# Matmuls on 48 of 64 rows and columns of a tile: the delta-rule state in a DeltaNet and SwiGLU kernel

## The chip, the cores and the metric

The kernel runs on one core of one Trainium2 chip. The metric is the device time of one execution in microseconds (us), as the median of several runs.

## What is computed

Two layers follow each other. The first is a DeltaNet recurrence over 768 positions for 4 batches x 8 heads with head size D = 48; its outputs, put side by side, are the 3072 rows of 384 that a SwiGLU feed-forward layer (384 to 1536 and back) takes, after an RMS normalization. Everything is float32.

```python
k_n = k / (norm(k, axis=-1) + 1e-06)
state = zeros((B, H, D, D))
for t in range(S):
    kt, vt, bt = k_n[:, :, t], v[:, :, t], beta[:, :, t, None]
    y[:, :, t] = einsum('bhd,bhde->bhe', q[:, :, t], state)
    v_old = einsum('bhde,bhd->bhe', state, kt)
    state = state + bt[..., None] * einsum('bhd,bhe->bhde', kt, vt - v_old)
...
x = y.transpose(0, 2, 1, 3).reshape(B * S, H * D)
xn = x / sqrt(mean(x * x) + 1e-06) * rms_g
g = xn @ w_gate
out = (g * sigmoid(g) * (xn @ w_val)) @ w_out
```

## The kernel before, in words

**Chunks.** The 768 positions are cut into NCH = 12 chunks of C = 64. Within a chunk the recurrence becomes matrix products: the inverse of a triangular matrix of each head is built (`prep`, lines 577 to 815), partly with matmuls, partly by a substitution on VectorE (lines 693 and 699) fed by DMAs that turn the layout over DRAM. Then `recur(c)` (lines 818 to 1030) does the part that needs the state: `on_state` (lines 834 to 844) multiplies the transposed keys `kt` by the state, line 854 subtracts that from the values, `mr` (line 886) applies the inverse and gives `u_`, `on_state` is used once more for the queries `qt`, `pu` (line 900) adds what lies within the chunk, and `ku` (lines 1011 to 1019) forms keys-transposed times `u_`, which line 1028 adds to `state` (in chunk 0, line 1030 copies it there).

**Heads and tiles.** There are 32 heads (batch x head). `k2`, `q2` and `state` hold two heads per free index, one on partitions 0 to 63 and one on 64 to 127. For the keys the partition is the position in the chunk, and a head's 48 values lie in DP = 64 columns of which the last 16 are set to zero once at the start (line 375). `turn` (line 509) transposes keys and queries on TensorE, so in `kt` and `qt` each head has 64 partitions, of which the last 16 hold these zeros. The state of a head is 48 columns on 64 partitions; its last 16 partitions hold zeros because the padded columns of K do.

**The matmuls concerned.** `ku` is 32 matmuls per chunk, for chunks 0 to 10: stationary operand `kn[rows, x_]` (64 positions x 64 columns), moving operand `u_[rows, x_]` (64 x 48), output on 64 partitions x 48 columns. `on_state` is 32 matmuls per call, called twice per chunk for chunks 1 to 11: stationary `t[rows, u, ...]` (64 rows x 64 positions), moving `state[rows, 2u+g]` (64 rows x 48), output 64 x 48. Both use TensorE as four tiles of 64 x 64: the loops' two innermost indices walk through the four combinations of upper or lower rows and upper or lower columns, and the two banks that a call fills belong to the upper and the lower rows.

**The feed-forward layer.** Chunks 0 and 1 are computed plainly (`ffn_plain`, lines 1064 and 1046). For later chunks the products are formed with fewer multiplications out of sums of blocks (`ffn`, line 1157 with sums on VectorE in line 1167; `down`, line 1214). In the first 125 us the weights arrive as 64-bit numbers and are turned into float32 on ScalarE and VectorE (`weights`, lines 440 to 480).

**The order of the work.** Each step is entered with `P.add(engine, duration, function, priority, ...)`. The planner (`Plan`, lines 60 to 243) simulates the engines with these written durations, tries 60 orders and issues the best one, engine by engine[...]. The durations are written numbers: 0.98 us for `ku` (line 1022) and for each `on_state` (lines 851 and 859). Before 70 us idle TensorE time is filled with dummy products (line 1312).

Of the kernel before, what the change touches and what calls it, by code (L numbers as in the profile page):

```python
# [246 lines left out]
def kernel(  # L247
# [17 lines left out]
    nc = tc.nc  # L265

    B, H, S, D = q.shape
# [12 lines left out]
    def sbt(name, shape, n=None, dt=FP32):  # L280
        if n is None:
            return sb.tile(shape, dt, name=name)
        return [sb.tile(shape, dt, name=f"{name}{i}") for i in range(n)]
# [45 lines left out]
    u_ = sbt("u", [128, 16, D])  # L329
# [212 lines left out]
    def kkeys_(c):  # L542
        return [("k2", c % NK, 0), ("k2", c % NK, 1)]
# [274 lines left out]
    def recur(c):  # L818
# [3 lines left out]
        kn = k2[c % NK]  # L822
# [7 lines left out]
        if c:  # L830

            psk, psq = [Group(), Group()], [Group(), Group()]

            def on_state(t, ps):
                for x_ in range(4):
                    for g in range(2):
                        for d in range(2):
                            for bb in range(2):
                                rows, u, n = slice(64 * d, 64 * d + 64), 4 * bb + x_, 96 * x_ + 48 * g
                                nc.tensor.matmul(  # L840
                                    ps[d].t[64 * bb : 64 * bb + 64, n : n + 48],
                                    t[rows, u, 64 * g : 64 * g + 64],
                                    state[rows, 2 * u + g],
                                )

            def by_d(t, d):

                return t.rearrange("s (x d n) -> s x d n", x=4, d=2)[:, :, d]

            P.rows = 64  # L850
            P.add("PE", 0.98, lambda: on_state(kt[ikq], psk), pr, r=ktk + sk, w=psk + rk, ps=psk, size=128)
            P.rows = 128
            for d in range(2):
                P.add("DVE", V(384), lambda d=d: nc.vector.tensor_tensor(  # L854
                    out=by_d(r_.rearrange("s h e -> s (h e)"), d), in0=by_d(vt.rearrange("s h e -> s (h e)"), d),
                    in1=psk[d].t[:, 0:DM].rearrange("s (x n) -> s x n", x=4), op=ALU.subtract,
                ), pr, r=vk + [psk[d]], w=[("r", d)], last=psk[d])
            P.rows = 64
            P.add("PE", 0.98, lambda: on_state(qt, psq), pr, r=qk + sk, w=psq, ps=psq, size=128)
            P.rows = 128  # L860
            for d in range(2):
                P.add("ACT", A(384), lambda d=d: nc.scalar.copy(
                    by_d(yn.rearrange("s p n -> s (p n)"), d), psq[d].t[:, 0:DM].rearrange("s (x n) -> s x n", x=4)
                ), py, r=[psq[d]], w=[("yn", p) for p in range(2)], last=psq[d])
# [44 lines left out]
        def uk(h):  # L909
            return [("u", bb, p) for bb in range(2) for p in h]  # L910
# [97 lines left out]
        if c < NCH - 1:  # L1008
            pss = [Group(), Group()]

            def ku():
                for b in range(B):
                    for j in range(2):
                        for d in range(2):
                            for g in range(2):
                                rows = slice(64 * g, 64 * g + 64)
                                x_ = 4 * b + 2 * j + d
                                n = 48 * (2 * b + j)
                                nc.tensor.matmul(pss[g].t[64 * d : 64 * d + 64, n : n + 48], kn[rows, x_], u_[rows, x_])  # L1019

            P.rows = 64
            P.add("PE", 0.98, ku, py + 2, r=kkeys_(c) + [("k2p", c % NK)] + uk((0, 1)), w=pss, ps=pss, size=128)
            P.rows = 128
            for g in range(2):
                dst = state[:, g:16:2]
                src = lambda g=g: pss[g].t[:, 0:DM].rearrange("s (u e) -> s u e", e=D)
                if c:
                    P.add("DVE", V(384), lambda dst=dst, f=src: nc.vector.tensor_tensor(out=dst, in0=dst, in1=f(), op=ALU.add), py + 2, r=[pss[g]], w=[("st", g)], last=pss[g])
                else:
                    P.add("ACT", A(384), lambda dst=dst, f=src: nc.scalar.copy(dst, f()), py + 3, r=[pss[g], ("xp", 0), ("xp", 1)], w=[("st", g)], last=pss[g])  # L1030
# [315 lines left out]
```

## Time and profile before

| what | value |
|---|---|
| median of 3 runs | 718.07 us (716.91 to 720.38) |
| the profiled execution, its own time | 720.75 us |
| its span, first to last instruction | 719.0 us |
| TensorE (PE) busy | 701.6 us, 98% of the span |
| PE weight loads (PEld) busy | 652.8 us |
| VectorE (DVE) busy | 553.8 us, 77% |
| ScalarE (ACT) busy | 314.3 us, 44% |
| mean granted TensorE clock | 0.993 |
| matmul records of line 1019 (`ku`) | 704, busy 12.8 us |
| matmul records of line 840 (`on_state`) | 2 x 704, busy 12.6 and 12.5 us |

A float32 matmul stands in the trace as two pairs of a weight load (LDWEIGHTS, engine PEld) and a MATMUL (engine PE), so the 32 matmuls of one call are 64 records. Records overlap: a MATMUL record lasts about 218 ns while the next one starts some nanoseconds later, so the time that a group takes is read from where the next group starts, not from the mean of one record. A shape such as `64*64 64x48` is active rows * active columns of the stationary operand, then rows x columns of the moving operand.

### The profile page before, as it was taken

Reading aid. Unit: us, or ns where it says so; the run is one execution under the profiler, and the core shown is the slowest. Engines: PE = TensorE matmul, PEld = TensorE weight load, DVE = VectorE, ACT = ScalarE, POOL = GpSimd, SP = SyncE. Lnnn points to the kernel's source line nnn. Section 1 sums busy time; section 2 is a strip of 40 time slices with the busy share of each in tenths; the row PEclk is TensorE's granted clock in tenths of the full one; section 3 lists DMA queues with packets and bytes.
Section 4 is the critical chain, followed back from the end, with each engine's and each line's share of the span. In section 5 each row is a group of like instructions: output and inputs, shape, how many; then the busy total and the mean of one; then the engine's idle time right before and its main releaser. Section 6 shows DMA issues by size and latency. Waiting matters only on the chain.

```text
span 719.0 us, 23540 instructions
## 1 busy us (share of the span) xinstructions
PE 701.6 (98%) x10178; PEld 652.8 (91%) x10178; DVE 553.8 (77%) x1128; ACT 314.3 (44%) x732; POOL 152.1 (21%) x150
## 2 busy tenths in 40 slices
PE   8988999999999999999999999999999999999997
PEld 7787877777799999998999999999999999999997
DVE  4898989998967958946967967975968958847473
ACT  5514544232345436354345255355355354344331
POOL 4200307004314132203213303203203221000000
PEclk9998999999999999999999999999999999999999
DMA  8867698141154261242234253253152061040000
GB/s 172 208 127 169 141 251 233 23 66 43 35 87 80 39 111 27 46 73 59 57 58 78 44 95 55 40 86 65 38 106 48 13 115 28 13 65 2 23 1 23
DMA packets 210071, 54.68 MB, mean 76 GB/s; under 512 B 199216, under 2 KB 202288, under 8 KB 209968
## 3 DMA queue, kind: packets, MB, share of 16 engines
q1 hardware_dynamic: 205120, 52.26, 36.4%
q8 instruction: 80, 1.31, 0.8%
q10 hardware_dynamic: 4848, 0.92, 0.7%
q14 instruction: 23, 0.19, 0.1%
HBM read 40.83 MB, written 12.32 MB: 74 GB/s over the span
## 4 chain that ended last, share of the span: by engine, by line
PE 79%; DVE 12%; DMA 4%; issue 2%; SPq 1%; POOL 1%; ACT 1%; ACTq 0%; DVEq 0%; POOLq 0%
PE bank L1157 36%; PE bank L1214 19%; PE bank L1064 6%; PE bank L1046 3%; PE bank L532 3%; PE bank L840 2%; PE bank L509 2%; DVE acc L699 2%; DMA more<-in_moe_w_gate_dram 2%; PE bank L799 2%; PE bank L886 1%; PE bank L1019 1%; PE bank L900 1%; DVE w_in L480 1%; DVE acc L693 1%
## 5 line engine op out<-in xcount | busy, mean ns | idle before, releaser
L1167 DVE TENSOR_TENSOR tmp<-tmp,bank 128x512 f32<-128x512 f32 x180 | 122.0, 685 | 85.9 <-PE bank L1157 75.9
L1157 PE MATMUL bank<-xf,w_in 128*128 128x128 f32 x1440 | 181.5, 277 | 0.2 <-DVE tmp L1167 0.2
L1157 PEld LDWEIGHTS bank<-xf,w_in 128*128 128x128 f32 x1440 | 169.8, 192 | 2.6 <-DVE tmp L1167 0.6
L1157 PE MATMUL bank<-xf,more 128*128 128x128 f32 x960 | 124.7, 277 | 0.0
L1157 PEld LDWEIGHTS bank<-xf,more 128*128 128x128 f32 x960 | 115.6, 192 | 1.7 <-DVE tmp L1167 0.4
L1169 ACT COPY tmp<-bank 128x512 f32<-128x512 f32 x120 | 68.5, 584 | 82.1 <-PE bank L1157 57.2
L699 DVE TENSOR_REDUCE acc<-acc 128x30 f32<-128x90 f32 (+4 forms) x180 | 85.1, 473 | 6.2
L1173 ACT ACTIVATE tmp<-tmp 128x256 f32<-128x256 f32 x120 | 49.7, 417 | 87.9 <-DVE tmp L1167 87.5
L693 DVE TENSOR_TENSOR acc<-acc,at 128x60 f32<-128x60 f32 (+4 forms) x180 | 63.4, 352 | 8.7 <-POOL at L676 5.9
L1214 PE MATMUL bank<-wo_sb,hf 128*128 128x192 f32 x360 | 63.8, 328 | 0.0
L1174 DVE TENSOR_TENSOR hf<-tmp 128x256 f32<-128x256 f32 x120 | 51.8, 443 | 13.0 <-ACT tmp L1173 11.7
L1214 PEld LDWEIGHTS bank<-wo_sb,hf 128*128 128x128 f32 x360 | 58.2, 190 | 0.3
L646 POOL TENSOR_TENSOR at<-at,beta_b 128x1024 f32<-128x1024 f32 x10 | 25.6, 2555 | 146.1 <-DMA at<-dkk 146.1
L554 POOL TENSOR_TENSOR knrm<-ksum,half 128x16 f32<-128x16 f32 x12 | 35.9, 2991 | 33.4 <-DVE ksum L553 33.4
L720 POOL COPY acc<-acc 128x128 f32<-128x128 f32 x40 | 17.1, 458 | 116.9 <-DVE acc L699 116.1
L1312 PE MATMUL bank<-ident 128*128 128x128 f32 x298 | 40.3, 296 | 1.4 <-POOL ident masks.py:199 1.4
L1312 PEld LDWEIGHTS bank<-ident 128*128 128x128 f32 x298 | 38.1, 209 | 2.5 <-POOL ident masks.py:199 1.4
L1046 PE MATMUL bank<-wo_sb,hf 128*128 128x384 f32 x96 | 34.3, 491 | 0.3 <-DVE r L854 0.3
L1064 PE MATMUL bank<-xf,w_in 128*128 128x256 f32 x144 | 33.6, 382 | 0.0
L1064 PE MATMUL bank<-xp,w_in 128*128 128x256 f32 x144 | 33.4, 383 | 0.0
L1064 PEld LDWEIGHTS bank<-xf,w_in 128*128 128x128 f32 x144 | 26.8, 190 | 4.9
L1064 PEld LDWEIGHTS bank<-xp,w_in 128*128 128x128 f32 x144 | 26.7, 190 | 4.4 <-issue 0.2
(164 smaller groups left out, 1047.9 us busy)
## 6 DMA issues: line engine op xcount, KB each, us to landing
at<-dkk SPq DMA_DIRECT2D x23, 256.0 KB, 4.0
q<-in_q_dram SPq DMA_DIRECT2D x24, 192.0 KB, 3.8
more<-in_moe_w_gate_dram SPq DMA_DIRECT2D x6, 768.0 KB, 6.0
more<-in_moe_w_val_dram SPq DMA_DIRECT2D x6, 768.0 KB, 7.2
more<-in_moe_w_out_dram SPq DMA_DIRECT2D x6, 768.0 KB, 8.4
vt<-in_v_dram SPq DMA_DIRECT2D x24, 192.0 KB, 4.2
out_dram<-tmp SPq DMA_DIRECT2D x48, 96.0 KB, 2.2
k<-in_k_dram SPq DMA_DIRECT2D x23, 192.0 KB, 4.2
```

What stands on the lines that cost most here:

```text
L554: P.add("POOL", 2.95, lambda: nc.gpsimd.tensor_tensor(out=knrm[i2], in0=ksum[i2], in1=half, op=ALU.pow), pn, r=[("ksum", i2), "half"], w=[ ...
L693: nc.vector.tensor_tensor(out=acc[:, 1:3, 0:n, j + 2 : W].rearrange("p a i t -> p i a t"), in0=acc[:, old, 0:n, j : j + 2, None].to_broadc ...
L699: nc.vector.tensor_reduce(out=acc[:, new, 0:n, j + 2 : W], in_=acc[:, lo : lo + 3, 0:n, j + 2 : W].rearrange("p a i t -> p i t a"), axis=A ...
L1046: nc.tensor.matmul(po[p].t[:, 0:DM], hf[:, spot(f), 128 * p : 128 * p + 128], wo_sb[:, spot(f)], start=(f == f0), stop=(f == f1 - 1), skip ...
L1064: nc.tensor.matmul(ps.t[:, TOK * side : TOK * side + TOK], w_in[:, side, h_, 3 * t + i_, n : n + 128], x_[:, 2 * t : 2 * t + 2].rearrange( ...
L1157: nc.tensor.matmul(g.t[:, 128 * z : 128 * z + 128], fac[:, side, 128 * f : 128 * f + 128], xf[:, xs], start=(begin and z == 0), stop=False ...
L1167: P.add("DVE", V(512), lambda t=t, g=g: nc.vector.tensor_tensor(out=t, in0=t, in1=g.t, op=ALU.add), -1, r=[g], w=[tk], last=g)
L1169: P.add("ACT", A(512), lambda t=t, g=g: nc.scalar.copy(t, g.t), -1, r=[g], w=[tk], last=g)
L1173: P.add("ACT", A(256), lambda t=t: nc.scalar.activation(out=t[:, 0:256], in_=t[:, 0:256], func=ACTF.Silu), -1, w=[tk])
L1174: P.add("DVE", V(256), lambda t=t, f0=f0, p=p: nc.vector.tensor_tensor(out=hf[:, spot(f0) : spot(f0) + 2, 128 * p : 128 * p + 128], in0=t[ ...
L1214: nc.tensor.matmul(g.t[:, 0:192], a_[:, f], b_[:, f], start=(begin and f == 0), stop=(f == 5), skip_group_check=True)
L1312: nc.tensor.matmul(warm[:, 0:128], ident, ident)
```

## The change

`ku` takes 48 columns of K instead of 64 as its stationary operand and writes 48 instead of 64 partitions of the bank. `on_state` contracts over 48 rows instead of 64: both the transposed keys or queries and the state are read on partitions 0 to 47 and 64 to 111. Its stationary operand still has 64 columns, and its output is as before. The padding of `k2` and `q2` is still set to zero, the transposes still turn 64 columns, and lines 1028 and 1030 still move all 128 partitions into `state`; the 16 partitions after each head's 48 then hold whatever the bank held, and no matmul reads them.

```diff
@@ on_state @@
-                                rows, u, n = slice(64 * d, 64 * d + 64), 4 * bb + x_, 96 * x_ + 48 * g
+                                rows, u, n = slice(64 * d, 64 * d + D), 4 * bb + x_, 96 * x_ + 48 * g
                                 nc.tensor.matmul(
                                     ps[d].t[64 * bb : 64 * bb + 64, n : n + 48],
                                     t[rows, u, 64 * g : 64 * g + 64],
@@ ku @@
-                                nc.tensor.matmul(pss[g].t[64 * d : 64 * d + 64, n : n + 48], kn[rows, x_], u_[rows, x_])
+                                nc.tensor.matmul(pss[g].t[64 * d : 64 * d + D, n : n + D], kn[rows, x_, 0:D], u_[rows, x_])
```

The instruction lists of the two kernels have the same length and order on all five engines, with the same waits. They differ in 1056 matmuls: 352 of line 1019 with the narrower stationary operand and output, 704 of line 840 with fewer rows. In both lists these matmuls are assigned to tiles of 64 x 64 at the same positions.

## The prediction, made before the changed kernel ran

> **What bounds the kernel now.** I read the page's busy table first, then the table by stretches of time, then the chain of work that ended last, and last the groups by shape.
>
> ```profile
> PE 701.6 (98%) x10178; PEld 652.8 (91%) x10178; DVE 553.8 (77%) x1128; ACT 314.3 (44%) x732; POOL 152.1 (21%) x150
> ```
>
> TensorE is busy 98% of the span. Overlapped records can hide idle spots in such a share, so the table by stretches says where it holds:
>
> ```profile
> 60.00:128.00 68.00, 64.88 (x1189) 52.66 (x1187) 62.39 (x98) 35.78 (x84) 20.66 (x13) 0.97 0.77 185
> 128.00:200.00 72.00, 72.00 (x637) 55.45 (x638) 66.23 (x133) 21.20 (x51) 17.44 (x17) 1.00 0.23 42
> 200.00:500.00 300.00, 298.55 (x4804) 289.26 (x4803) 225.47 (x478) 142.71 (x335) 72.61 (x71) 1.00 0.37 65
> 500.00:719.00 219.00, 214.35 (x2885) 208.84 (x2883) 153.27 (x327) 89.65 (x216) 29.20 (x34) 1.00 0.22 40
> ```
>
> The first number after the stretch's length is PE's busy time, the third VectorE's. From 128 us on PE is idle for moments only, until the last outputs are stored. Before 128 us VectorE is the fuller engine (62.4 of 68 us) with weight conversion, and PE's time there has dummy products in it (line 1312). So a microsecond of PE work saved after 128 us should come off the end, and one saved before is likely hidden. The chain agrees: from 60 to 128 us it is mostly VectorE conversion, after that mostly PE.
>
> Now the matmuls that change. These are pieces of the chain (start, length, both in us):
>
> ```profile
> 371.30 10.02 PE bank L1157 x88
> 381.32 2.01 PE bank L840 x128
> 398.63 1.08 PE bank L1019 x64
> 400.65 2.15 PE bank L1214 x12
> ```
>
> A call of 64 records takes 1.08 us; two calls of `on_state` one behind the other take 2.01, so the second costs 0.93 us. Four records on four tiles are one round, a call is 16 rounds, and 0.93 / 16 is 58 ns a round. The single starts in the trace say the same: four MATMULs start within 20 ns, the next four 58.3 ns later (58.29 to 58.36 in nearly every call of lines 1019, 840, 886, 900 and 532). Only the first round of a call behind 128-row work is longer, 93 to 94 ns. What sets 58.3? Line 532 moves 64 columns and lines 1019 and 840 move 48, at the same 58.3; all load 64 stationary columns. Line 1157 (128 stationary, 128 moving) takes 111.66 ns from start to start within a group (10.02 us / 88 = 113.9 ns with the entry into it). From 64 to 128 columns is 53.3 ns, 0.833 ns a column, with 5 ns over. Lines with moving operands wider than their weights follow another line: 162.5 ns at 192 (line 1214), 322.5 at 384 (line 1046), 55.83 a round for line 775 with 64 moving and 32 stationary: 0.833 ns a column plus 2.5. So a round takes the longer of 0.833 x P + 5 (P stationary columns) and 0.833 x N + 2.5 (N moving columns). The changed lines sit on the first.
>
> ```profile
> L1019 PEld LDWEIGHTS bank<-u,k 64*64 64x64 f32 x704 | 11.4, 134 | 2.4 <-issue 2.1
> L775 PEld LDWEIGHTS bank<-m1bd,wsum 128*32 128x32 f32 x32 | 0.5, 109 | 0.5 <-issue 0.5
> L751 PEld LDWEIGHTS bank<-ident,mt 32*32 32x32 f32 x64 | 1.0, 107 | 2.1 <-issue 2.1
> ```
>
> In these groups by shape the mean load is 134 ns for 64 columns, and 109 and 107 for 32 columns, whether 128 or 32 rows are active: columns count, rows hardly.
>
> **What the Trainium skill says.** "TensorE: Matmul & The Clock Gate", section "LDWEIGHTS (loading the stationary operand)": the load lasts P / 1.2 ns with P the columns, and the contraction rows don't matter. The trace agrees on both: 0.833 ns a column, and the 109 against 107 above. The same page, Part 3 "The mechanism": loads are pulled ahead of running matmuls on other row groups. The trace agrees, since a 134 ns load fits into a 58 ns round only if loads overlap. "TensorEngine Tiling (Array Packing)", "Restrictions": the active columns must not exceed the tile's column limit. 48 stays under 64, and the compiled list keeps 64 x 64 tiles, so the four-way packing should stay. The same page, "Instruction Overhead": about 60 cycles per matmul, so that 1 to 60 moving columns cost the same. Here starts on different tiles lie 6.7 ns apart, so this is no bound on a round of four (4 x 6.7 = 27 ns). No run here shows active columns fewer than the tile's.
>
> **The change part by part.**
>
> *ku with 48 stationary columns.* P falls from 64 to 48: 0.833 x 48 + 5 = 45.0 ns a round; the moving bound is 0.833 x 48 + 2.5 = 42.5, so weights still set it. Each round saves 13.3 ns. A call has 16 rounds, so 16 x 13.3 = 0.21 us (0.20 if the last round already waits for the 64-column load of the next call in the same mode). There are 11 calls, 704 records / 64. By their starts, two lie before 128 us (68.1 and 108.4 us) and nine after, as the records of line 1019 per stretch confirm:
>
> ```profile
> 0.00:128.00 128.00, 2.49 (x128) 2.23 (x128) 0.96 0.77 183
> 128.00:719.00 591.00, 10.33 (x576) 9.22 (x576) 1.00 0.30 53
> ```
>
> 576 / 64 = 9 calls on the path: 9 x 0.21 = 1.9 us. The two early calls, 0.4 us, I cost at nothing: behind the first PE runs 16 dummy products, and behind the second VectorE converts weights until about 125 us. If that cover were gone the gain would be 2.3 us. Bounds: 0 if the load takes the tile's 64 columns whatever is active, 2.3 if all of it lands. I take 1.9, because every load in this trace follows its column count.
>
> *ku writing 48 partitions.* Nothing: the moving operand streams 48 columns as before. Lines 1028 and 1030 read the same number of elements, 0.54 us each for line 1028, with undefined numbers on 32 partitions that no matmul reads.
>
> *on_state with 48 rows.* P stays 64 and N stays 48, so the round stays 58.3 and the 22 calls cost the same: 0. Its bounds: a gain if rows counted in the load as columns do, 13.3 x 16 = 0.21 us for each of the 18 calls after 128 us (1152 records / 64), 3.8 us; a loss if a partly filled tile gave up its overlap (below). I take 0, from the row comparison above.
>
> *Order and waits.* The five instruction lists are the same in order and waits. No DMA, no wait and no step is moved, and the plan's written 0.98 us is unchanged. An earlier end of `ku` is passed on to line 1028, which waited for it 0.4 us in all, so little comes from there.
>
> *Does the saving reach the end?* After 128 us PE idles 1.45 us inside an `on_state` call at 334 us, where nothing shown is waited for, 0.17 us at 502 us behind VectorE, and 0.22 us at 636 us behind a DMA. The wait at 502 us hangs on a chain of DMA issues, a landing and GpSimd and VectorE steps, which began with a PE product at 474 us and so moves with it. If each of the two waits swallowed the saving of one call (0.21), 1.5 us would be left.
>
> Sum: the profiled execution of 720.75 us goes to 718.85 (span 719.0 to 717.1). It is 2.7 us above the median; taking 1.9 from the median 718.07 gives **716.2 us**.
>
> **Rivals.**
>
> *The load takes the tile's columns.* Every load in this trace fills its tile's columns (128, 64 or 32), so the trace can't tell active columns from tile columns. If a 64-wide tile is loaded in 64 steps anyway, nothing changes: 718.1 us. For it: no counterexample here. Against it: the skill's formula speaks of element count.
>
> *Partly filled tiles lose the overlap: slower.* If 48 rows or 48 columns in a 64 x 64 tile made TensorE wait for each load, every round would look like the first of a call, 93.5 ns instead of 58.3: 35 ns x 15 rounds x 27 calls (9 + 18) after 128 us = 14.2 us, thus 732 us. For it: no partial tile has been seen here. Against it: the tile assignment is unchanged, and loads of different shapes all overlap. It decides from the point where the 18 x 15 = 270 later rounds of `on_state` cost over 1.9 us more, that is 7 ns a round, 65 instead of 58.3.
>
> *Rows count too.* 1.9 + 3.8 = 5.7 us, thus 712.4 us. The 109 and 107 ns loads speak against it.
>
> **How the numbers follow.** Forecast 716.2: chance 0.68. Tile columns, 718.1: 0.19. Lost overlap, 732: 0.09. Rows too, 712.4: 0.04. The runs before lie from 1.2 us below to 2.3 above their median, and 0.5% of 718 is 3.6 us, about what a measurement of this kernel can tell from no change. Faster by more than that: the rows case, and a share of 0.04 by scatter around the forecast, 0.08. Slower: lost overlap and 0.02 of scatter, 0.11. Between: 0.81. The range takes in the forecast with its scatter, the nothing case with its own, and the 2.3 us bound: 714.0 to 720.0. It leaves out the lost overlap and the rows case, 0.13, and some scatter. The forecast's own range is 714.5 to 718.
>
> **What would show it.** A call of line 1019 in the chain at 0.86 to 0.88 us instead of 1.08, rounds of 45 ns, and its mean load near 121 ns; line 840 still 1.08 and its rounds 58.3. If line 1019 stays at 1.08, tile columns count. If line 840 grows beyond 1.2, the overlap is lost. The prediction is wrong beyond its range if a partial tile behaves unlike a full one, or if a new stall such as the 1.45 us one appears several times.

## The result, and the profile after

| | before | after |
|---|---|---|
| median of 18 runs each | 718.26 us (716.91 to 721.08) | 716.61 us (715.95 to 718.5) |
| the profiled execution, its own time | 720.75 us | 717.67 us |
| its span | 719.0 us | 716.0 us |

The ratio is 0.9975 with a 95% interval of 0.9965 to 0.9984: a gain of 1.8 us (1.1 to 2.5) by the ratio, 1.65 us by the medians. The forecast was 1.9.

The weight loads and matmuls of line 1019, two lines from the profile before and two from the profile after (in this view: count, then the shortest, median and longest record in ns, the first and last start in us, the shape):

```profile
L1019 PEld LDWEIGHTS bank<-u,k x704: 129/135/135, 68.1 to 612.4; 64*64 64x64 f32 x176
L1019 PE MATMUL bank<-u,k x704: 199/218/254, 68.1 to 612.5; 64*64 64x48 f32 x176
L1019 PEld LDWEIGHTS bank<-u,k x704: 116/122/122, 69.1 to 609.7; 64*48 64x48 f32 x176
L1019 PE MATMUL bank<-u,k x704: 205/205/240, 69.1 to 609.7; 64*48 64x48 f32 x176
```

The median load fell from 135 to 122 ns for 16 columns fewer, and the median MATMUL record from 218 to 205. Line 840 before and after:

```profile
L840 PEld LDWEIGHTS bank<-state,qt x704: 129/135/135, 78.5 to 629.7; 64*64 64x64 f32 x176
L840 PEld LDWEIGHTS bank<-state,qt x704: 129/135/135, 79.1 to 626.9; 48*64 48x64 f32 x176
L840 PE MATMUL bank<-state,qt x704: 205/218/253, 79.1 to 627.0; 48*64 48x48 f32 x176
```

Its shape shows 48 active rows, and its durations are what 64 rows had, 135 and 218 ns. The records of line 1019 by stretch:

```profile
0.00:128.00 128.00, 1.87 (x128) 1.62 (x128) 0.96 0.75 183
128.00:716.00 588.00, 8.41 (x576) 7.30 (x576) 1.00 0.30 53
```

After 128 us the nine calls are busy 8.41 instead of 10.33 us: 1.92 us less. In the chain, the call that took 1.08 us at 398.63 us before now reads:

```profile
396.54 0.86 PE bank L1019 x64
397.40 0.95 PE bank L532 x64
398.35 2.15 PE bank L1214 x12
```

0.86 us against 1.08, and what follows it keeps its length. By the single starts a round takes 45.0 ns in all eleven calls, and the first round 80 instead of 93 to 94. From the start of a call to the next line's start it is 0.865 instead of 1.078 us (0.755 instead of 0.968 where another call in 64 x 64 tiles follows): 0.213 us less in every call but the first one. That one took 1.274 us before, because TensorE stood still in it for 0.2 us, and 0.865 after.

TensorE's longest unexplained wait after 128 us (waiter, releaser, total us, times, longest us; "issue" means that nothing shown is waited for), first before, then after:

```profile
PE bank L840 <- issue: 1.4, 1, 1.4
```

```profile
PE bank L840 <- issue: 0.9, 1, 0.9
PE bank L1214 <- DVE xp L1206: 0.2, 1, 0.2
```

The wait inside a call of `on_state` is shorter, and line 1214 has a new one of 0.2 us for VectorE, at 461 us.

Since TensorE's order is unchanged, the two profiles can be laid over each other record by record. From the first line 1046 record at the end of the conversion stage (128.00 us before, 127.28 after) to the last record TensorE is 2.35 us shorter after. The nine calls of line 1019 give 1.920 us of it, 0.213 each. The shorter wait of line 840 at 334 us gives 0.57, and two waits that are gone (502 us, for VectorE, and 637 us, for a DMA) give 0.27 and 0.29. The other way go 0.45 us at 461 to 463 us and 0.22 at 568 to 570 us, both at products of line 1214 whose operand VectorE makes in line 1206. Which of these belong to the change is told by the runs below. The stage before 128 us is 0.7 us shorter in this pair, and the experiments don't let me ascribe that to the change.

### The profile page after: what moved, and what is told of

It is laid out like the page before. It is cut to its first block, busy times and chain, and to the rows that moved or that the text cites. A ratio compares the mean times of both kernels' runs of the same rounds, so it can differ in the third digit from the quotient of the medians.

```text
span 716.0 us, 23540 instructions
## 1 busy us (share of the span) xinstructions
PE 701.5 (98%) x10178; PEld 652.9 (91%) x10178; DVE 553.6 (77%) x1128; ACT 314.0 (44%) x732; POOL 152.7 (21%) x150
## 4 chain that ended last, share of the span: by engine, by line
PE 80%; DVE 15%; DMA 2%; issue 2%; SPq 1%; ACT 0%; DVEq 0%
PE bank L1157 38%; PE bank L1214 18%; PE bank L1064 6%; PE bank L1046 3%; PE bank L840 3%; PE bank L532 2%; DVE acc L699 2%; PE bank L509 2%; PE bank L799 2%; PE bank L886 2%; DVE acc L693 1%; DMA beta_b<-in_beta_dram 1%; PE bank L900 1%; DVE w_in L480 1%; PE bank L775 1%
## 5 line engine op out<-in xcount | busy, mean ns | idle before, releaser
L1312 PE MATMUL bank<-ident 128*128 128x128 f32 x298 | 42.0, 304 | 1.4 <-POOL ident masks.py:199 1.4
```

The lines of the kernel that those rows point to most:

```text
L1312: nc.tensor.matmul(warm[:, 0:128], ident, ident)
```

## The experiments

The theory: a round of four small matmuls takes the longer of 0.833 ns x stationary columns + 5 and 0.833 ns x moving columns + 2.5; rows are free; TensorE time after 128 us is all on the path. The rivals: rows matter, alone or with columns; the new round has another floor; TensorE's time is partly hidden. A ratio below is to the kernel before in the same series of runs. A difference to the changed kernel sets medians of different series side by side; the kernel before had 718.26 to 718.93 us in them.

**One half at a time.** Changed kernel with line 839 put back (`e1`), and with line 1019 put back (`e2`):

```diff
-rows, u, n = slice(64 * d, 64 * d + D), 4 * bb + x_, 96 * x_ + 48 * g
+rows, u, n = slice(64 * d, 64 * d + 64), 4 * bb + x_, 96 * x_ + 48 * g
```

> Only the first half of the change: the state's update with 48 stationary columns, on_state on 64 rows as before (the last 16 rows of each head's state are then bank leftovers that meet zeros of K and Q). If the gain is all the narrower weight load: rounds of line 1019 at 45.0 ns, line 840 at 58.3 ns, time below the kernel before by 9 x 0.21 = 1.9 us, ratio near 0.9974. If fewer rows in on_state are what helps: line 1019 still at 45 but the time like before, ratio 1.000. If only both together help: somewhere between.

Measured: 717.13 us against 718.81 us of before, ratio 0.9978 (0.9965 to 0.9990). Rounds of line 1019 at 45.0 ns, of line 840 at 58.3. The first half gives what the whole change gives, within the intervals.

```diff
-nc.tensor.matmul(pss[g].t[64 * d : 64 * d + D, n : n + D], kn[rows, x_, 0:D], u_[rows, x_])
+nc.tensor.matmul(pss[g].t[64 * d : 64 * d + 64, n : n + 48], kn[rows, x_], u_[rows, x_])
```

> Only the second half: on_state on 48 rows, the state's update with 64 columns as before. If columns alone set a round: line 840 at 58.3 ns a round, its 22 calls at 1.08 us, ratio 1.000. If fewer rows help although the records don't show it (say by ending a call earlier for VectorE): ratio 0.998 or lower.

Measured: 718.49 us, ratio 0.9994 (0.9977 to 1.0011), in which no change can be told. Line 840 by stretch, first in the profile before, then in the profile of this run:

```profile
0.00:128.00 128.00, 4.54 (x256) 4.10 (x256) 0.96 0.77 183
128.00:719.00 591.00, 20.08 (x1152) 18.31 (x1152) 1.00 0.30 53
```

```profile
0.00:128.00 128.00, 4.54 (x256) 4.10 (x256) 0.97 0.77 184
128.00:715.00 587.00, 20.08 (x1152) 18.31 (x1152) 1.00 0.29 53
```

The busy times are equal. Going from 64 to 48 rows doesn't count, and this is no longer an argument from other lines. A warning goes with this run: its profiled span is 715.5 us, 3.5 below that of before, though its median is not lower. Laid over the kernel before, its nine calls of line 1019 give 0.002 us; 0.67, 0.24 and 0.25 us come at the waits at 334, 502 and 637 us, and the rest before 128 us. So these three differences come without the shorter calls, and are no part of what they gain. Two others go with the shorter calls: laid over the kernel before in the same way, the changed kernel, `e1` and `e3` each lose 0.08 us at 463 us and 0.22, 0.22 and 0.27 us at 568 us, and this run loses nothing there. The remaining 0.37 us of the changed kernel at 461 us is 0.22 in `e3` and absent in `e1`, so the shorter call alone doesn't bring it.

**Below 48 columns.** With 48 moving columns the two bounds cross at 45 stationary columns, so 40 tells them apart (`e3`):

```diff
-slice(64 * d, 64 * d + D), 4 * bb + x_
+slice(64 * d, 64 * d + 40), 4 * bb + x_
...
-pss[g].t[64 * d : 64 * d + D, n : n + D], kn[rows, x_, 0:D]
+pss[g].t[64 * d : 64 * d + 40, n : n + D], kn[rows, x_, 0:40]
```

> The state's update with 40 stationary columns and on_state on 40 rows: leaves out the last 8 of the 48 key and query columns of the state's part. By the two bounds, the load would allow 0.833 x 40 + 5 = 38.3 ns a round, the 48 moving columns 0.833 x 48 + 2.5 = 42.5. If a round takes the longer of the two: 42.5 ns, line 1019's call at 0.82 us, and against the changed kernel only 9 x 16 x 2.5 ns = 0.36 us less, ratio to before near 0.9969. If the load alone sets it: 38.3 ns, 0.96 us less than the changed kernel, ratio near 0.996. If partial tiles have another floor: 45 ns still.

Measured: 42.5 ns a round in all eleven calls, 716.26 us, ratio 0.9956 (0.9940 to 0.9971). In its chain and among its loads:

```profile
345.75 0.82 PE bank L1019 x64
```

```profile
L1019 PEld LDWEIGHTS bank<-u,k x704: 109/113/113, 68.4 to 608.9; 64*40 64x40 f32 x176
```

The load got shorter still (122 to 113 ns), yet the round stopped at 42.5: the 48 moving columns bound it now. Both bounds of the prediction are shown. In time the further 0.36 us is within the intervals.

**Is early TensorE time hidden?** The prediction costed the two calls before 128 us at nothing. Written out four times (`e5`):

```diff
-                for b in range(B):
+                for b in [b for _ in range(4 if c < 2 else 1) for b in range(B)]:
```

> The changed kernel, with the two early calls of the state's update (chunks 0 and 1) written out four times over, each repeat overwriting the same numbers: 2 x 3 x 16 x 45 ns = 4.3 us of additional TensorE work before 128 us. If early TensorE time is hidden behind VectorE's weight conversion, as the prediction has it: under 0.9 us more than the changed kernel (a fifth). If TensorE's queue passes it on: 4.3 us more, ratio near 1.0035 to the kernel before. Half and half would be 2 us.

Measured: 728.35 us, ratio 1.0127 (1.0095 to 1.0159), 11.7 us more than the changed kernel. Neither number. TensorE's timeline of this run around the first of these calls (start us, length us, then the group; in brackets the idle time before it):

```profile
68.15 0.47 PE L1019 MATMUL bank<-u,k 64*48 64x48 f32 x19
69.13 1.65 PE L1019 MATMUL bank<-u,k 64*48 64x48 f32 x128 [0.52 <-issue]
73.14 2.29 PE L1019 MATMUL bank<-u,k 64*48 64x48 f32 x109 [2.35 <-issue]
```

and around the end of the conversion stage:

```profile
122.48 0.66 PE L509 MATMUL bank<-ident,q 128*128 128x128 f32 x4
127.39 1.01 PE L509 MATMUL bank<-ident,q 128*128 128x128 f32 x4 [4.25 <-issue]
```

The call stands still twice with nothing shown that it waits for, and line 509 once. The DMA packets of a queue that brings instructions say what it is. They carry 16 KB each, and one ended at 67.63, one at 71.68 and one at 125.94 us; TensorE went on at 69.13, 73.14 and 127.39, that is 1.50, 1.46 and 1.45 us later. The same holds for the wait inside line 840 near 334 us: 1.34 us after such a packet in the kernel before, 1.36 in the changed one, 1.42 to 1.47 in `e1` to `e3`.

The position of these waits in TensorE's instruction stream settles the cause. There are 80 such packets in the profiles with 20356 records of weight loads and matmuls, 83 with 21124 (this run) and 84 with 21508 (`e6`): one packet for 256 records. Counted over all records of TensorE, its sequencer's included, every wait of over 0.15 us for which nothing is shown comes after the 193rd record or a multiple of 256 later: 26 of 26 waits, in eleven of the twelve profiles. And additional records move them. The wait inside line 840 near 334 us stands in the six profiles of kernels in this order that have no records added ahead of it, or 768 (this run, 3 x 256); it is gone where 384, 80 and 48 were added (`e6`, `e8` and `e9` below). So a new packet begins at these places, and TensorE stood still until it had come.

The long standstills cost more than their length. The stretch around the end of the third one in this run, then the same stretch in the changed kernel (the third number from the end is the granted clock, as a share of full speed):

```profile
125.00:131.00 6.00, 3.61 (x11) 3.07 (x11) 5.93 (x4) 0.59 (x1) 5.92 (x4) 0.50 0.24 46
```

```profile
125.00:131.00 6.00, 4.37 (x17) 2.97 (x18) 5.76 (x15) 2.18 (x4) 0.15 (x1) 1.00 0.35 66
```

The clock was halved there, and for 3.4 us behind the second standstill too: a round of the fourth copy took 80 instead of 45 ns. So 7.1 us of standstill in three waits and a halved clock come on top of 4.3 us of work, and part of it all is covered.

The experiment tested instruction delivery as much as TensorE time, so it was made again with few, long instructions (`e8`):

```diff
-                for b in range(B):
+                for b in ([nc.tensor.matmul(pss[0].t[:, 384:512], ident, ident) for _ in range(10 if c < 2 else 0)], range(B))[1]:
```

> The changed kernel with ten dummy products (128x128 of the identity, into unused columns of the bank) ahead of each of the two early calls: 2 x 20 records x 0.112 us = 4.5 us of TensorE time before 128 us, in few instructions, so that no wait without a releaser should come of it as it did with the early calls written out four times. If early TensorE time is hidden, as the prediction had it: under 0.9 us more than the changed kernel's 716.6 us. If TensorE's queue passes it on: 4 to 5 us more, ratio near 1.004 to the kernel before.

Measured: 720.75 us, ratio 1.0036 (1.0018 to 1.0055), 4.1 us more than the changed kernel's 716.61 (4.4 by the ratios, uncertain by some 1.5), so not hidden. The chain of this run between 60 and 128 us, which was VectorE's conversion before, is now TensorE's through and through up to 114 us; four of its pieces:

```profile
75.01 1.53 PE bank L1312 x12
76.54 3.89 PE bank L1064 x18
80.43 1.08 PE bank L840 x64
81.51 1.02 PE bank L509 x8
```

In this profile the conversion stage ended at 130.00 us. In the five kernels with this order and no additional work it ended anywhere from 125.65 to 128.00 us, so 4.5 us of work moved it by 2.0 to 4.35 us. How far VectorE leads there can't be read from single profiles better than that: by 2.5 us at most, perhaps by nothing. Whether a saving of 0.4 us was hidden is not shown.

**Is late TensorE time all on the path?** The nine later calls written out twice (`e6`):

```diff
-                for b in range(B):
+                for b in [b for _ in range(2 if c > 1 else 1) for b in range(B)]:
```

> The changed kernel, with each of the nine later calls written out twice: 9 x 16 x 45 ns = 6.5 us of additional TensorE work after 128 us. If that time is all on the path to the end: 6.5 us more than the changed kernel, ratio near 1.0065 to the kernel before. If TensorE's waits for VectorE give part of it back (the changed kernel shows new ones of 0.2 and 0.1 us): 5.5 to 6.3 us more.

Measured: 725.87 us, ratio 1.0103 (1.0082 to 1.0123), 9.3 us more than the changed kernel: above both numbers. TensorE's timeline of this run at one of three such places:

```profile
455.15 1.66 PE L1019 MATMUL bank<-u,k 64*48 64x48 f32 x128
456.63 0.54 PE L532 MATMUL bank<-qt,kt 64*64 64x64 f32 x22
458.66 0.85 PE L532 MATMUL bank<-qt,kt 64*64 64x64 f32 x42 [1.49 <-issue]
```

and its sum among the waits:

```profile
PE bank L532 <- issue: 3.8, 3, 1.6
```

The waits of 1.55, 1.49 and 0.75 us end 1.48, 1.32 and 1.53 us after an instruction packet ended. With 6.5 us of work they make 10.3, about a microsecond more than the time measured. Laid over the changed kernel, two things give time back: the wait in line 840 near 334 us is gone (1.1 us), and delays of lines 1214 and 1157, whose operands VectorE makes, are shorter by 0.9 us at 461, 500 and 567 us. Other delays at 336 and 367 us cost 0.9 again. With long instructions in place of many short ones (the same line as in `e8`, with `4 if c > 1 else 0`; `e9`):

> The same with four dummy products ahead of each of the nine later calls: 9 x 8 x 0.112 = 8.0 us after 128 us, 8.9 us if each call in 64x64 tiles has a change of tiling more in front of it. If TensorE time after 128 us is all on the path and the excess of the run with doubled calls came from waits for instructions: 7.5 to 9 us more than the changed kernel, without new waits that no releaser is shown for. If something else amplifies late TensorE time: over 11 us.

Measured: 724.31 us, ratio 1.0084 (1.0064 to 1.0105), 7.7 us more than the changed kernel for 8.0 us of work. In its profile the stretch from the end of the conversion stage is 7.7 us longer too (596.4 against 588.7), and no wait stands at the added products. But the wait for instructions is not gone, it has moved; this run has, in place of the one in line 840:

```profile
PE bank L775 <- issue: 1.2, 1, 1.2
```

That is at 384 us. Against the changed kernel the moved wait adds some 0.35 us, and the delays behind VectorE at 461, 500 and 567 us are shorter by 0.9, as in `e6`. So TensorE's time after 128 us is on the path, less about a tenth that shorter waits for VectorE give back.

**The plan told the truth.** Could the planner use the shorter call? The changed kernel with 0.77, 0.85 and 0.93 us in line 1022 instead of 0.98:

```diff
-            P.add("PE", 0.98, ku, py + 2, ...
+            P.add("PE", 0.77, ku, py + 2, ...
```

> The changed kernel, with the planner told the shorter call: 0.77 instead of 0.98 us. The order of all engines comes out anew (the plan searches with random steps), so 0.21 us of truth a call is mixed with another draw of the order. If the plan's order is already as good as the model's accuracy allows: within 0.5% of the changed kernel, either side. If the true price matters to the order: faster than the changed kernel by over 2 us.

> The changed kernel with 0.85 us told to the planner for the state's update. If the loss with 0.77 was a bad draw of the order and not the price: anywhere from 1.5% slower to 0.5% faster than the changed kernel, not ordered by the price. If a price nearer the old one is better: between the changed kernel (716.6 us) and 724 us.

> The same with 0.93 us told to the planner. If draws decide: unrelated to the run with 0.85 us. If the price decides: closer to the changed kernel than that one.

Measured: 724.15 us (ratio to before 1.0071, 1.0052 to 1.0089), 731.07 us (1.0181, 1.0157 to 1.0205) and 733.13 us (1.0206, 1.0154 to 1.0257). The first is neither within 0.5% of the changed kernel nor faster, and the second is 2.0% slower than it, outside both of its ranges. The true price lost least of the three, and the prices nearer the old one lost more (the last two can't be told apart), so nearness to the old price is no help. As each price was tried with one order only, price and draw are not separated; what is shown is that each price gives another order, and that the one at 0.98 is better than these three. A part of the loss shows at once in TensorE's records: with 0.93 it idles from 166.85 to 173.47 us ahead of line 900, with 0.85 and 0.77 for 4.6 and 2.7 us around the same time, where the changed kernel has no gap; with the gaps of 6.6 and 4.6 us came 6.8 and 3.4 us at a granted clock of 0.5. None of these versions beats the changed kernel.

## Why the prediction was right

*ku's round at 45.0 ns.* Right to the digit: 45.0 measured, 0.213 us a call, 1.920 us over nine calls. What the trace of before could not tell, whether the P in the Trainium skill's price ("TensorE: Matmul & The Clock Gate", "LDWEIGHTS (loading the stationary operand)") is the active columns or the tile's, is settled: 16 and 24 active columns fewer in a 64-wide tile shorten the load from 135 to 122 and 113 ns. The trace agrees with that price in the slope, 0.833 ns a column of a round, not in the length of a record: P / 1.2 would be 53 ns for 64 columns. A matmul has as many output partitions as stationary columns, so no run parts the narrower load from the narrower output; that the load records shrank speaks for the load. `e3` shows that the second bound, from the moving columns, is real too (42.5 ns).

*on_state at no cost.* Right: 58.3 ns a round with 48 and with 64 rows, and `e2` gives 0.9994. The row comparison that it rested on was weaker than it looked, since the larger groups with 32 columns and 128 rows had mean loads of 114 and 115 ns (lines 799 and 775), against 107 with 32 rows; `e2` shows what it could not.

*No loss of overlap in partly filled tiles.* Right: the rival at 732 us and the tile-columns rival at 718.1 are refuted by the rounds of `e1`. The first round of a call shrank as well, from 93 to 80 ns.

*The saving reaches the end.* Right in the main. The allowance that two waits swallow one call each, 1.5 us, came near by luck: of the two waits that it named, the one at 502 us is in none of the four profiles laid over the kernel before, and the one at 636 us is in `e1` alone, with 0.12 us. What takes time back in every kernel with short calls is 0.22 us or more at 568 us and 0.08 at 463, at products of line 1214 whose operand VectorE makes, which the prediction had at nothing. 1.92 less 0.30 is 1.62, against 1.65 by the medians; the interval of the gain, 1.1 to 2.5, is much wider than that agreement. The profiled pair fell by 3.1 us and not by the 1.9 forecast for it: the rest is the waits that differ without the change, and the stage before 128 us.

*The early calls are hidden.* This step isn't supported as it was put. `e8` shows that 4.5 us of additional TensorE work before 128 us are not hidden, so dummy products behind a call are no proof of cover: they are instructions in TensorE's queue like others, and are issued whether or not there is time. That the 0.4 us of these two calls was hidden, as costed, stays open. A run that would settle it would have to tell 0.4 us apart, and the narrowest interval here, from 18 runs of each kernel, is 1.4 us wide.

## What to carry to other kernels

Before narrowing an operand, find out from the spacing of starts which of the two widths sets the round: here it is the longer of stationary and moving columns, each with its own constant, and 40, 48 or 64 rows cost the same. Then count the saving in every call that lies where TensorE leads, and look for what the next engine in line takes back; here it was 0.30 of 1.92 us. Where the planned order is a search result, leave its prices alone if the order is already good: three new draws cost 7 to 17 us, and the change was worth 1.7.

## What the runs showed of the hardware that was not expected

TensorE can outrun the queue that brings its instructions. All 26 waits of over 0.15 us without a releaser ("issue") stand where a new packet of 256 records begins, and ended 1.2 to 1.7 us after a packet had landed. With boundaries and packets paired in order, TensorE went on sooner than 1.22 us after its packet at none of 955 boundaries in twelve profiles. Matmuls in 64 x 64 tiles use up instructions fast: a call of 48 columns issues its 64 loads and 64 MATMULs in 0.86 us. `e6` stood still behind two such calls in three places of nine, and in `e5` 128 short matmuls with nothing between were followed by 2.35 us of standstill. A matmul added or removed moves the boundaries behind it. That narrower operands make standstills longer, since the same instructions are used up sooner, would follow, but it is not shown: the wait near 334 us was 1.45 and 0.78 us with the long calls, 0.88, 1.18 and 1.15 with the short ones.

A long standstill can also slow what follows. With the waits of 2.35 and 4.25 us in `e5`, and of 4.6 and 6.6 us in the kernels told 0.85 and 0.93 us, came stretches of 3.4 or 6.8 us at a granted clock of 0.50, where the changed kernel has 1.00; the wait of 2.7 us in the kernel told 0.77 brought none.
